# Decode attention with a gated MLP: which queue starts w1, x, b1 and b2, and when wq is issued

## The chip, the cores and the metric

The kernel runs on one core of a Trainium2 chip. The metric is the device time of one execution in microseconds (us). Data comes from HBM through 16 DMA engines that are shared by all queues of the core; SyncE (SP in the profile) and ScalarE (ACT) each issue transfers onto a queue of their own, `q1` and `q10` in the profile's numbering. That `q10` is ScalarE's can be seen from its contents: in the whole execution it holds 8 packets, which are the four rows of x, b1 and b2 and their four completions.

## What is computed

```python
x = A_x                                   # (2, 1, 512)
xn = layernorm(x)
q = xn @ wq                               # 32 heads of 128
p = softmax(q . k_cache / sqrt(128))      # k_cache, v_cache: (2, 32, 8192, 128) f32
s = (p . v_cache) @ wo
g = silu(gelu(layernorm(xn) @ w1 + b1) @ w2 + b2)   # w1: (512, 1376), w2: (1376, 512)
out = x + s * g
```

All is float32. The two caches are 512 MiB together, wq and wo 8 MiB each, w1 and w2 2.75 MB each.

## The kernel before

The caches are walked in 32 tiles of two heads: a K tile and a V tile are 128 partitions by 64 KB (8 MiB) each. VectorE multiplies a K tile with the broadcast query and reduces it (two passes), TensorE and ScalarE make the softmax, and TensorE multiplies the V tile. K has two buffers (`KBUF`, lines 107 to 109), V one (`VB`). `take("SP", "p_k")` and `take("SP", "p_free")` (lines 311 to 325) are SyncE's waits for a buffer to be free before it issues the next tile. Every operation is recorded by the helper `op` (lines 47 to 60), so the profile shows line 51 for nearly all of them; tiles tell them apart. The names `w1_sb`, `w2_sb`, `x_sb`, `xn`, `wo_sb` and others are views of the three large buffers `big`, and `wq_sb` is the second K buffer before it gets its first K tile, so their rows read `big<-in_B_w_dram`, `big<-in_A_x_dram` and so on.

Ahead of the loops stands a prologue, which the change touches. Lines 200 to 202: ScalarE issues x (two rows of 2 KB), b1 (one row of 5.5 KB) and b2 (one row of 2 KB). Lines 203 to 205: SyncE issues the last 96 lines of w2 (2 KB each), w1 (128 rows of 22,016 bytes, one for each partition) and wq (128 rows of 64 KB); line 212 the first K tile, line 213 the rest of w2. None of these waits for anything. VectorE clears PSUM banks and makes small masks out of an identity (lines 228 to 246), then runs `layernorm` (lines 251 to 260): statistics and their aggregation on VectorE, a square root on ScalarE, a reciprocal and the normalization on VectorE. Line 262 normalizes x, waiting for x's transfer; line 263 normalizes that once more for the MLP. TensorE transposes both, computes the hidden layer from w1, then q from wq (lines 435 to 441, event `pq`), spreads q over the partitions, and computes the gate from w2.

SyncE's later transfers hang on this: the second K tile (line 302) waits for `pq` and for wq's transfer, since it overwrites wq; the first V tile (lines 308 and 309) waits for the gate, since it overwrites w1, w2 and the rest of the third buffer. An engine's instructions run in their order, so a waiting SyncE issues nothing that is written behind the wait.

At the end come wo in eight transfers (lines 326 to 329), the last products, and the output's transfer.

Of the kernel before, what the change touches and what calls it, by code (L numbers as in the profile page):

```python
# [13 lines left out]
class Program:  # L14
# [32 lines left out]
    def op(self, eng, method, *args, waits=(), sig=None, by=1, quiet=False, **kwargs):  # L47
        need = self.need(eng, waits)
        for name, v in need[:-1]:
            self.engines[eng].wait_ge(self.sem(name), v)  # L50
        ins = getattr(self.engines[eng], method)(*args, **kwargs)  # L51
        for name, v in need[-1:]:
            ins._wait_ge(self.sem(name), v)
        if quiet:
            return None
        name = sig or "own_" + eng
        by = 16 if method == "dma_start" else by
        ins.then_inc(self.sem(name), by)
        self.counts[name] += by
        return name, self.counts[name]  # L60


def decode_kernel(nc, x, kc, vc, wq, wo, w1, b1, w2, b2, out):
    P = 128
# [18 lines left out]
    NF = F // P  # L83
# [12 lines left out]
    op, wait, take = pr.op, pr.wait, pr.take  # L96

    def sb(shape, name):
        return nc.alloc_sbuf_tensor(name, list(shape), F32).ap()
# [12 lines left out]
    def boot(p, n):  # L112
        a = used[0]
        used[0] += n
        assert used[0] <= KP * DH
        return big[2][:p, a:a + n]

    w1_sb = boot(P, ND * F).rearrange("p (c f) -> p c f", f=F)
    QN = big[2][:BH, 2 * 512:2 * 512 + N * DH].rearrange("h (n d) -> h n d", d=DH)
    w2_sb = boot(P, (NF + 1) * D).rearrange("p (c n) -> p c n", n=D)  # L120
    x_sb = boot(B, D)
    xn = boot(B, D)
    y = boot(B, D)
    b2_sb = boot(1, D)
    b1_sb = boot(1, F)
# [5 lines left out]
    wq_sb = big[1].rearrange("p (c n) -> p c n", n=H * DH)  # L131
# [59 lines left out]
    def pe(name):  # L191
        return "pe_setup", PE_EVENTS.index(name) + 1

    def pe_n(name, n):
        return name, n + 1

    t = {}


    t["x"] = op("ACT", "dma_start", x_sb, x.rearrange("b s d -> (b s) d"), sig="d_x")  # L200
    t["b1"] = op("ACT", "dma_start", b1_sb, b1[None, :], sig="d_b1")
    t["b2"] = op("ACT", "dma_start", b2_sb, b2[None, :], sig="d_b2")
    op("SP", "dma_start", w2_sb[:FT, NF, :], w2[NF * P:, :], sig="d_w2")
    op("SP", "dma_start", w1_sb, w1.rearrange("(p c) f -> p c f", p=P), sig="d_w1")
    op("SP", "dma_start", wq_sb, wq.rearrange("(p c) n -> p c n", p=P), sig="d_wq")

    def load_k(n, *waits):
        sems, cuts = ([f"d_k{n % U}", "d_kl"], HALVES) if n == N - 1 else ([f"d_k{n % U}"], (0, KP))
        for name, (c0, c1) in zip(sems, zip(cuts, cuts[1:])):
            op("SP", "dma_start", KBUF[n % U][:, c0:c1], kf[n][:, c0:c1], sig=name, waits=waits)  # L210

    load_k(0)
    t["w2"] = op("SP", "dma_start", w2_sb[:, :NF, :], w2[:NF * P, :].rearrange("(p c) n -> p c n", p=P), sig="d_w2")


    op("POOL", "memset", ones, 1.0)
# [12 lines left out]
    for k in (7, 6, 1, 2, 4, 0):  # L229
# [13 lines left out]
                  op=ALU.add)  # L243
    t["sel"] = op("DVE", "tensor_copy",
                  sel[:, HP:].rearrange("p (b j r) -> p b j r", b=B, r=HG)[:, :, :QT, 0], by_row[:, :B, :],
                  waits=[t["sel0"]])
# [4 lines left out]
    def layernorm(dst, src, name, after):  # L251
        st = sb([B, nc.vector.BN_STATS_DIM], f"st_{name}")
        mv = sb([B, nc.vector.BN_AGGR_DIM], f"mv_{name}")
        sd = sb([B, 2], f"sd_{name}")
        a = op("DVE", "bn_stats", st, src, waits=[after])
        a = op("DVE", "bn_aggr", mv, st, waits=[a])
        c = op("ACT", "activation", sd[:, 0:1], mv[:, 1:2], AF.Sqrt, bias=eps_t, scale=1.0, waits=[a])
        c = op("DVE", "reciprocal", sd[:, 1:2], sd[:, 0:1], waits=[c])
        return op("DVE", "tensor_scalar", dst, src, mv[:, 0:1], sd[:, 1:2], op0=ALU.subtract, op1=ALU.mult,
                  waits=[a, c])  # L260

    t["xn"] = layernorm(xn, x_sb, "xn", t["x"])
    t["y"] = layernorm(y, xn, "y", t["xn"])
    t["xnT"] = op("DVE", "tensor_copy", xnT, pxn.rearrange("p (c b) -> p c b", b=B), waits=[pe("xnT")])
    t["yT"] = op("DVE", "tensor_copy", yT, py.rearrange("p (c b) -> p c b", b=B), waits=[pe("yT")])
# [4 lines left out]
    c = op("DVE", "tensor_mul", gu, gh, gh, waits=[a])  # L270
    c = op("DVE", "tensor_scalar", gu, gu, GELU_A, 1.0, op0=ALU.mult, op1=ALU.add, waits=[c])
    c = op("DVE", "tensor_mul", gu, gu, gh, waits=[c])
    c = op("ACT", "activation", gu, gu, AF.Tanh, scale=GELU_C, waits=[c])
    c = op("DVE", "scalar_tensor_tensor", gu, gu, 1.0, gh, op0=ALU.add, op1=ALU.mult, waits=[c])
# [8 lines left out]
    for part, n0, n1 in (("first", 0, NPB), ("rest", NPB, N)):  # L283
# [3 lines left out]
                           waits=[t["qall"], t["mine"]])  # L287
# [15 lines left out]
    for b in range(B):  # L303
        t["x4"] = op("SP", "dma_start", x4[HB * b::R, :], x[b, 0].rearrange("(j n) -> j n", n=P), sig="d_x4",
                     waits=[t["x4m"]])
# [49 lines left out]
    with nc.scalar.Fori(0, N // U) as i:  # L355
        for u in range(U):
# [4 lines left out]
            for s in range(U):  # L361
# [11 lines left out]
                   waits=[t["th"], t["pool"]])  # L373
# [8 lines left out]
                 op=ALU.mult, waits=[t["rl"], t["on0"], pe_n("p_oa", 0)])  # L382
    t["wide"] = op("ACT", "copy", o4, pw, waits=[pe_n("p_w", 0)])
    a = op("DVE", "scalar_tensor_tensor", res, acc, 0.5, gate, op0=ALU.mult, op1=ALU.mult,
           waits=[pe_n("p_acc", 0), t["gate"]])
    t["res"] = op("DVE", "tensor_add", res, res, x4, waits=[a, t["x4"]])
    t["out"] = op("SP", "dma_start", out.rearrange("b s (j n) -> j (b s) n", n=P), res[::HB, :], sig="d_out",
                  waits=[t["res"]])
# [42 lines left out]
    for k in range(NH):  # L431
        n = min(QT, NF + 1 - k * QT)
# [9 lines left out]
    for n in range(NG // QT):  # L442
        for hh in range(HG):
# [3 lines left out]
               waits=[t["sel"], t["qnat"]], sig="pqa" if last else None)  # L447

    for g in range(N // NPB):
        mm(PB[g % len(PB)], sides, QN[:, g * NPB:(g + 1) * NPB, :].rearrange("h n d -> h (n d)"),  # L450
           waits=[t["side"], t["QN rest" if g else "QN first"]] + ([t[f"Q{QH}"]] if g >= len(PB) else []),
           sig=f"pb{g}")
    for f in range(NF + 1):
# [3 lines left out]
           waits=[t["hT"], t["w2"], t["mem6"]])  # L457
    mm(pg[R * (QT - 1):R * (QT - 1) + B, :], ones[:1, :B], b2_sb, start=False, stop=True, waits=[t["b2"]], sig="pg")
    for j in range(QT):
        mm(pgate[R * j:R * j + MB, :], mod_b[:, :MB], g_nat[:, j * P:(j + 1) * P], waits=[t["g"], t["mod_b"]],  # L460
           sig="pgate" if j == QT - 1 else None)
# [64 lines left out]
    for b in range(B):  # L526
        h = slice(b * H, (b + 1) * H)
        mm(OA[:, b, :OC], Z[:, h].rearrange("p h r -> p (h r)"), mod, waits=[t["Z"]],
           sig="p_oa" if b == B - 1 else None)
    unread(1)  # L530
    for i, (c0, c1) in enumerate(zip(WO_CUTS, WO_CUTS[1:])):
        for c in range(c0, c1):
            after = [t["on"], t["mem"], (f"d_wo{i}", 16)]
            if c < WIDE:
                j = c % QT
                mm(pw[R * j:R * j + MB, :], on[:, :, c], wo_sb[:, c, :], start=c < QT, stop=c + QT >= WIDE,
                   waits=after, sig="p_w" if c == WIDE - 1 else None)
# [7 lines left out]
        if c1 == OC - 2:  # L545
            for j in range(QT):
                mm(acc[R * j:R * j + MB, :], mod[:, :MB], o4[:, j * P:(j + 1) * P], start=False, stop=False,
                   waits=[t["wide"]])
# [26 lines left out]
```

## Time and profile before

| | us |
|---|---|
| median of 3 runs (1299.70 to 1301.15) | 1300.71 |
| time of the profiled execution | 1299.53 |
| its span | 1298.2 |

1.3 us of the profiled execution lie around its span. Over the span the 16 DMA engines moved 559.30 MB at 431 GB/s, VectorE was busy for 87% and TensorE for 36%. In the rows, "SPq" and "ACTq" are the issuing side of SyncE and ScalarE, `<-` behind a time names what ended an engine's idle time, and a DMA share of 1.00 is all 16 engines busy. The share of a very short window can pass 1, since a packet is counted where it begins.

### The profile page before, as it was taken

What the parts mean: (1) busy time and instruction counts of PE and PEld (TensorE: products, weight loads), DVE (VectorE), ACT (ScalarE), POOL (GpSimd) and SP (SyncE); (2) the same over time, 40 slices, a digit from 0 to 9 for tenths busy, and PEclk for the clock granted to TensorE, in tenths of its full rate; (3) what the DMA queues carried; (4) which work ended last, traced back from release to release, by engine and by line L of the source; (5) the groups of instructions that cost most, each with busy time, mean ns of one, the idle gap of its engine ahead of it and who ended that gap; (6) DMA issues with size and microseconds to landing.
All of it is one profiled execution on the core that took longest, in us unless ns stands there. A gap on an engine that the chain in (4) does not pass through costs nothing. (4 is left out here: it accounts for less than half of the span.)

```text
span 1298.2 us, 7420 instructions
## 1 busy us (share of the span) xinstructions
PE 465.6 (36%) x2958; PEld 150.8 (12%) x2958; DVE 1135.7 (87%) x171; ACT 81.1 (6%) x279; POOL 2.3 (0%) x15
## 2 busy tenths in 40 slices
PE   3813343323334322433322343322334321333338
PEld 1201111001111000111100111100111100111103
DVE  2599999988889988889988888988888988888991
ACT  1200000000000000000000000000000000000000
POOL 0000000000000000000000000000000000000000
PEclk8757766666776566677656767656776666677659
DMA  9999999999999999999999999999999999999998
GB/s 412 436 426 442 430 430 436 426 446 426 438 430 424 446 426 442 430 430 436 426 446 426 438 430 424 446 426 444 428 432 434 426 446 426 438 430 424 432 436 360
DMA packets 11241, 559.37 MB, mean 431 GB/s; under 512 B 1264, under 2 KB 1536, under 8 KB 1892
## 3 DMA queue, kind: packets, MB, share of 16 engines
q1 hardware_dynamic: 11228, 559.30, 99.7%
q8 instruction: 3, 0.05, 0.0%
q14 instruction: 2, 0.02, 0.0%
q10 hardware_dynamic: 8, 0.01, 0.0%
HBM read 559.30 MB, written 0.00 MB: 431 GB/s over the span
## 5 line engine op out<-in xcount | busy, mean ns | idle before, releaser
L51 DVE TENSOR_TENSOR big<-big,bank 128x16384 f32<-128x16384 f32 (+1 forms) x33 | 551.2, 16704 | 73.2 <-DVEq L45 73.2
L51 DVE TENSOR_REDUCE sc<-big 128x128 f32<-128x16384 f32 (+1 forms) x33 | 551.2, 16703 | 4.8
L51 PE MATMUL bank<-big,PZ 128*8 128x512 f32 x2048 | 293.0, 736 | 632.1 <-PEq L45 632.1
L51 PEld LDWEIGHTS bank<-big,PZ 128*8 128x8 f32 x2048 | 60.5, 103 | 837.3 <-issue 837.3
L51 PE MATMUL bank<-Q,ident 128*128 128x512 f32 (+2 forms) x198 | 79.8, 514 | 0.3 <-issue 0.3
L51 ACT COPY o<-bank 128x512 f32<-128x512 f32 x33 | 19.3, 586 | 887.3 <-ACTq L45 875.9
L51 PE MATMUL bank<-ident,MX 128*1 128x128 f32 x32 | 9.8, 308 | 132.8 <-PEq L45 132.8
L51 PE MATMUL bank<-mod,o 128*128 128x2 f32 x256 | 32.8, 250 | 27.4 <-PEq L45 27.4
L51 PEld LDWEIGHTS bank<-mod,o 128*128 128x128 f32 x256 | 31.0, 191 | 55.4 <-issue 55.4
L51 PEld LDWEIGHTS bank<-Q,ident 128*128 128x128 f32 x198 | 34.8, 205 | 16.5 <-issue 16.5
L51 ACT ACTIVATE PZ<-sc,bias 64x128 f32<-64x128 f32 x64 | 25.5, 399 | 6.6 <-ACTq L45 6.2
L51 DVE TENSOR_REDUCE nm<-bank 1x2 f32<-1x128 f32 x32 | 8.9, 279 | 19.4 <-DVEq L45 19.4
L51 DVE TENSOR_TENSOR big<-big,mine 64x512 f32<-64x512 f32 (+1 forms) x2 | 4.5, 2278 | 21.2 <-ACT big L51 21.2
L51 PEld LDWEIGHTS bank<-ident,MX 128*1 128x1 f32 x32 | 2.5, 79 | 157.8 <-issue 157.8
L51 ACT COPY bias<-bank 128x1 f32<-128x1 f32 x32 | 5.1, 159 | 220.2 <-ACTq L45 220.2
L51 PE MATMUL bank<-big,sides 64*128 64x512 f32 x16 | 12.8, 972 | 3.7 <-DVE big L51 3.7
L51 PE MATMUL bank<-nm,srow 1*64 1x1 f32 x128 | 10.4, 218 | 8.9 <-PEq L45 7.1
L51 DVE TENSOR_REDUCE MX<-sc 128x1 f32<-128x128 f32 x32 | 9.2, 286 | 4.7
L51 PE MATMUL bank<-big,xnT 128*2 128x512 f32 x64 | 9.0, 727 | 10.3 <-DMA big<-in_A_wq_dram 10.3
L51 ACT ACTIVATION_READ_ACCUMULATOR PZ<-sc,bias x64 | 11.8, 185 | 0.0
L51 PE MATMUL bank<-big,on 128*17 128x512 f32 (+1 forms) x88 | 10.8, 569 | 0.9 <-DMA big<-in_A_wo_dram 0.8
L51 DVE SCALAR_TENSOR_TENSOR res<-bank,gate 128x128 f32<-128x128 f32 x1 | 0.3, 291 | 11.9 <-PE bank L51 11.9
(80 smaller groups left out, 83.8 us busy)
## 6 DMA issues: line engine op xcount, KB each, us to landing
big<-in_A_k_cache_dram SPq DMA_DIRECT2D x2, 4096.0 KB, 35.9
big<-in_A_v_cache_dram SPq DMA_DIRECT2D x2, 4096.0 KB, 35.8
big<-in_B_w_dram SPq DMA_DIRECT2D x1, 2752.0 KB, 10.2
big<-in_B_w_dram SPq DMA_DIRECT2D x1, 2560.0 KB, 52.1
big<-in_A_wo_dram SPq DMA_DIRECT2D x1, 2560.0 KB, 15.0
big<-in_A_wo_dram SPq DMA_DIRECT2D x1, 2048.0 KB, 19.5
big<-in_A_wo_dram SPq DMA_DIRECT2D x1, 1536.0 KB, 22.7
big<-in_A_wo_dram SPq DMA_DIRECT2D x1, 1024.0 KB, 24.8
```

The costliest lines, as they stand in the source:

```text
L51: ins = getattr(self.engines[eng], method)(*args, **kwargs)
```

## The change

ScalarE issues one transfer only, w1, as its first instruction. SyncE issues w2's last lines as before, and behind them x, b1 and b2 on the same queue. wq, the first K tile and the rest of w2 move behind the first normalization in the program, still on SyncE's queue and in their old order, and wq gets a wait for that normalization's result `xn`. What is computed stays the same.

```diff
@@ -197,20 +197,17 @@
-    t["x"] = op("ACT", "dma_start", x_sb, x.rearrange("b s d -> (b s) d"), sig="d_x")
-    t["b1"] = op("ACT", "dma_start", b1_sb, b1[None, :], sig="d_b1")
-    t["b2"] = op("ACT", "dma_start", b2_sb, b2[None, :], sig="d_b2")
+    op("ACT", "dma_start", w1_sb, w1.rearrange("(p c) f -> p c f", p=P), sig="d_w1")
     op("SP", "dma_start", w2_sb[:FT, NF, :], w2[NF * P:, :], sig="d_w2")
-    op("SP", "dma_start", w1_sb, w1.rearrange("(p c) f -> p c f", p=P), sig="d_w1")
-    op("SP", "dma_start", wq_sb, wq.rearrange("(p c) n -> p c n", p=P), sig="d_wq")
+    t["x"] = op("SP", "dma_start", x_sb, x.rearrange("b s d -> (b s) d"), sig="d_x")
+    t["b1"] = op("SP", "dma_start", b1_sb, b1[None, :], sig="d_b1")
+    t["b2"] = op("SP", "dma_start", b2_sb, b2[None, :], sig="d_b2")
 
     def load_k(n, *waits):
...
-    load_k(0)
-    t["w2"] = op("SP", "dma_start", w2_sb[:, :NF, :], w2[:NF * P, :].rearrange("(p c) n -> p c n", p=P), sig="d_w2")
...
@@ -260,6 +257,9 @@
     t["xn"] = layernorm(xn, x_sb, "xn", t["x"])
+    op("SP", "dma_start", wq_sb, wq.rearrange("(p c) n -> p c n", p=P), sig="d_wq", waits=[t["xn"]])
+    load_k(0)
+    t["w2"] = op("SP", "dma_start", w2_sb[:, :NF, :], w2[:NF * P, :].rearrange("(p c) n -> p c n", p=P), sig="d_w2")
     t["y"] = layernorm(y, xn, "y", t["xn"])
```

## Rows read from the trace of the kernel before

**Rows 1.** The page: engines, DMA share in 40 slices, ScalarE's queue, w1's landing.
```profile
PE 465.6 (36%) x2958; PEld 150.8 (12%) x2958; DVE 1135.7 (87%) x171; ACT 81.1 (6%) x279; POOL 2.3 (0%) x15
DMA  9999999999999999999999999999999999999998
q10 hardware_dynamic: 8, 0.01, 0.0%
...
big<-in_B_w_dram SPq DMA_DIRECT2D x1, 2752.0 KB, 10.2
```

**Rows 2.** Windows by stage: window, length, engines' busy time, PEclk, DMA share, GB/s.
```profile
2.00:12.00 10.00, 1.09 (x8) 1.03 (x8) 6.73 (x23) 1.75 (x3) 0.91 (x5) 1.00 1.04 419
12.00:50.00 38.00, 22.09 (x141) 7.68 (x142) 5.57 (x8) 4.75 (x9) 0.00 (x0) 0.80 1.00 431
...
600.00:1230.00 630.00, 216.13 (x1399) 68.95 (x1392) 570.86 (x65) 35.23 (x130) 0.00 (x0) 0.67 1.00 433
```

**Rows 3.** Windows of the last transfers, columns as in Rows 2.
```profile
1293.00:1293.25 0.25, 0.25 (x8) 0.00 (x0) 0.00 (x0) 0.00 (x0) 0.00 (x0) 1.00 1.09 397
...
1293.75:1294.00 0.25, 0.06 (x5) 0.01 (x1) 0.00 (x0) 0.13 (x1) 0.00 (x0) 1.00 0.52 180
...
1294.50:1294.90 0.40, 0.40 (x24) 0.37 (x16) 0.00 (x0) 0.00 (x0) 0.00 (x0) 1.00 0.14 49
```

**Rows 4.** Timeline, K and V transfers: start, length, engine, line, what, idle before.
```profile
30.84 9.04 PE L51 MATMUL bank<-big,xnT 128*2 128x512 f32 x64 [10.26 <-DMA big<-in_A_wq_dram]
40.02 0.33 SPq L51 DMA_DIRECT2D big<-in_A_k_cache_dram  x1
65.76 0.34 SPq L51 DMA_DIRECT2D big<-in_A_v_cache_dram  x1
87.00 0.35 SPq L51 DMA_DIRECT2D big<-in_A_k_cache_dram  x1
95.09 9.35 PE L51 MATMUL bank<-big,PZ 128*8 128x512 f32 x64 [8.32 <-PEq L45]
```

**Rows 5.** Timeline of the prologue: the issues, and the first normalization.
```profile
0.74 0.55 ACTq L51 DMA_DIRECT2D big<-in_A_x_dram  x1
0.74 0.88 SPq L51 DMA_DIRECT2D big<-in_B_w_dram  x2
1.32 0.53 ACTq L51 DMA_DIRECT2D big<-in_B_b_dram  x2
1.66 1.94 SPq L51 DMA_DIRECT2D big<-in_A_wq_dram  x1
3.65 0.43 SPq L51 DMA_DIRECT2D big<-in_A_k_cache_dram  x1
5.72 0.68 DVE L51 BATCH_NORM_STATS2 st_xn<-big 2x6 f32<-2x512 f32 x1
7.15 0.53 DVE L51 TENSOR_SCALAR big<-big,mv_xn,sd_xn 2x512 f32<-2x512 f32 x1
12.08 5.59 PE L51 MATMUL bank<-big,yT 128*2 128x384 f32 x40 [0.35 <-DVE yT L51]
21.96 0.18 DVE L51 TENSOR_SCALAR hT<-gu 128x22 f32<-128x22 f32 x1
```

**Rows 6.** Queues (packets, MB, share) in 1.6 to 1.9, 4.9 to 5.1, 5.8 to 5.9.
```profile
q1 hardware_dynamic: 8, 0.02, 32.9%
q8 instruction: 1, 0.02, 30.2%
q10 hardware_dynamic: 4, 0.00, 5.1%
...
q1 hardware_dynamic: 6, 0.13, 154.3%
q10 hardware_dynamic: 1, 0.00, 2.6%
...
q1 hardware_dynamic: 1, 0.02, 51.1%
q10 hardware_dynamic: 1, 0.00, 0.6%
```

## What the change was predicted to do

> **What bounds the kernel now.** I read the page first: VectorE is busy for 87% of the span, but the 16 DMA engines stand at 9 in 39 of 40 slices, and in the last at 8 [rows 1]. The windows by stage say it more sharply: from the prologue to the end of the loops the DMA share is 1.00 or a little more, at 419, 431 and 433 GB/s [rows 2]. So nothing that an engine computes sets the time; the DMA engines do, from their first byte to the last of wo. The timeline shows why they never run dry in the loops. The second K tile is issued at 40.02 and the first V tile at 65.76; the next K tile goes onto the queue at 87.00, while the V tile before it is used only from 95.09 on [rows 4]. At 433 GB/s a tile of 8.39 MB takes 19.4 us, so each issue comes some 8 us before the engines would be idle. **Thus the rule for this change**: an instant in which a DMA engine idles ahead of wq is paid in full at the end, and one microsecond saved there is gained in full. Everything behind wq keeps its order: q's products start when wq has landed (30.84), the second K tile is issued behind them (40.02) [rows 4], and all of that moves with wq by the same amount, the queue being as full as before.
>
> **The DMA engines in the prologue before.** Issues start at 0.74 on both queues, x on ScalarE's and w2's last lines and w1 on SyncE's; wq is issued from 1.66 and the K tile from 3.65 [rows 5]. x is on the engines early: in 1.6 to 1.9 us ScalarE's queue has four of its eight packets, two rows and two completions [rows 6]. That is 0.86 to 1.16 us behind x's issue; I take 1.0 us from the start of an issue to its first packet. VectorE clears banks until 5.72 and then normalizes without any wait for x; the result is written at 7.15 + 0.53 = 7.68 [rows 5]. The chain from x to `xn` is 7.68 - 5.72 = 1.96 us. Ahead of wq lie w1 (2.82 MB), w2's last lines (0.20 MB) and some 0.03 MB of the rest: 3.05 MB, 7.3 us at 419 GB/s [rows 2]. From a first packet at about 1.7 this ends at 9.0 on average; w1's last row landed 10.2 us behind its issue at 0.74 to 1.18 [rows 1, 5], so the slowest engine ended at 10.9 to 11.4. For most engines I take **9.5**, an estimate nearer to the lower end, since few engines are late [rows 3]. wq's rows have long been queued by then, so no engine waits.
>
> **What the change costs, step by step.**
> (1) w1 on ScalarE's queue: one issue at 0.74 instead of three of 1.08 us together [rows 5]. w1's first rows come up to half a microsecond sooner, but w2's last lines now share the engines with them; the bytes ahead of wq are the same, so w1 is done at about 9.4, and this part is worth 0 to -0.3 us. The hidden layer begins at 12.08 behind the second normalization, not behind w1, so w1's landing isn't what it waits for [rows 5].
> (2) x behind w2's last lines. x's issue moves from 0.74 to 0.74 + 0.44 = 1.18, by half of the 0.88 us that the two issues took [rows 5]. That half microsecond is nothing by itself: x has until 5.72. What matters is how a DMA engine shares itself between w1's rows on one queue and the short rows on the other. Before, b2 stood in just that place: ScalarE's last issue ended at 1.32 + 0.53 = 1.85 [rows 5], and with the same 1.0 us (counted from the middle of that double issue, 1.59) its row would be due at about 2.6. Its row is in the window of 4.9 to 5.1, and its completion in the one of 5.8 to 5.9 [rows 6]. A row of w1 takes 22,016 bytes / (433 GB/s / 16) = 0.81 us on one engine; the completion thus came one w1 row behind the data that directly preceded it, and the data 2.4 us, or three such rows, late. I read this as one packet from each queue in turn. On the engines that carry x, SyncE's queue now holds six of w2's 96 lines (96 / 16), their completion, x's row and x's completion, that is nine packets, against eight rows of w1 (128 / 16) and a completion on ScalarE's. In turns, x's completion stands behind all eight rows of w1: about 1.7 + 1.2 (the first row, taken half as long again) + 7 x 0.81 + 8 x 0.08 = **9.2**. It can't be much later, since w1 is then done; it can be as early as 5.72 or sooner at no cost, if the short rows pass. I take 9.3.
> (3) The wait. `xn` is ready at 9.3 + 1.96 = 11.3; SyncE sees it some 0.1 later, issues wq, and the first packets follow 1.0 to 1.6 us behind (1.0 as above, and up to 0.6 more for the engine served last: in 1.6 to 1.9 only 8 packets of w2's lines had come to 16 engines [rows 6]). wq's rows so begin at 12.4 to 13.0 instead of about 9.5: **+2.9 to +3.5 us** for an engine that was early before. Queued behind the waiting wq on SyncE are the first K tile and the rest of w2; neither can fill the gap. b1 and b2 are ahead of it and are only 7.5 KB.
> (4) The restart. The engines stop and start again; how slow first rows are no row shows by itself. I bound it by 0 and the 0.8 us of one whole w1 row, and take nearly the middle, **+0.35**.
> (5) What the stop gives back. The engines don't end together: their share is 1.09 in 1293.00 to 1293.25, 0.52 in 1293.75 to 1294.00 and 0.14 in 1294.50 to 1294.90 [rows 3], so the last two or three end over a microsecond behind the bulk. One source of such a lag is seen in the prologue: an instruction load on `q8` takes one engine's time at 1.6 to 1.9 [rows 6]. As the engines never wait afterwards, a lag from the prologue is kept to the end. A stop before wq lets the late ones catch up. Bounds are 0 and 1.2 us; I take **-0.8**.
> The sum is 2.9 to 3.5, so 3.1, then + 0.35 - 0.8 - 0.15 = **+2.5 us**. On the profiled execution (1299.53) that is 1302.0; the median of the runs is 1.18 us higher, and on it the sum gives **1303.2**, +0.19%. What hides the rest: the hidden layer, its activation (`hT` done at 21.96 [rows 5]) and the second normalization all come 3.6 us later, but q's products wait for wq until 30.84 [rows 4], 8.9 us behind `hT`, and wq moves too.
>
> On the turns a rule of the Trainium skill speaks otherwise. The row on b2 shows one w1 row between b2's data and its completion, which follow each other on the same queue [rows 6]. DMA: Bandwidth & Descriptors, section "Queues, rings and completion order", says that an engine drains a whole packet, typically 9 to 17 descriptors, of one queue before it switches. By that rule the nine short packets ahead of and with x would be one turn, and the sum would be rival 1's instead of +2.5 us; b2's completion speaks against it, as data and completion would not have been parted.
>
> **Rivals.**
> *1. x passes w1, and nothing changes.* If the short packets of SyncE's queue go in one turn, or w2's lines are through before w1's first rows come, x is there by 2.7 to 5.7. Then `xn` is ready at 7.68 as before, wq is issued at about 7.8 and its rows queue from 8.8 to 9.4, just before w1 ends at 9.4. Shift -0.5 to +0.6 us, **1300.7**. For it: x's two rows are ready to go by 2.2 and need only 0.08 us each. Against it: b2 [rows 6].
> *2. Clearly slower: wq's issue itself is long.* The only issue of wq in the trace took 1.94 us, while K tiles with rows of the same size took 0.33 to 0.43 [rows 4, 5]. Before, that was hidden behind w1's 7 us; now nothing stands behind it. If the rows reach the engines only as the issue goes on, the last engine starts 1.5 us later than in (3), and the kernel takes +4 us, **1304.7**. The same happens if x's engine is one delayed by an instruction load. It decides from an issue above 0.9 us on. Against it: the length coincides with the instruction load that starts before 1.9, which the new order has long behind it when wq is issued.
> *3. Faster.* w1's earlier first rows (-0.3) and the engines' catching up (-0.8 at most), with x early enough that no gap arises: -0.6 to -1.1, **1299.8**. The catching up needs a stop, though, so both together are unlikely.
>
> **How the numbers follow.** About 0.2% of this kernel, 2.6 us, is what a measurement can tell from no change. My forecast has 0.60, with a range of its own from +1.6 to +3.3 us (1302.3 to 1304.0) from the bounds in (2) to (5); of it 0.26 lies above 2.6 us. Rival 1 has 0.20, rival 2 0.16, rival 3 0.04, of which 0.02 faster than 0.2% is already generous. Slower: 0.26 + 0.16 = 0.42; faster 0.02; same 0.56. The range goes from rival 1's lower part, 1300.2, to the middle of rival 2, 1304.8; outside are about 0.08 above and 0.07 below.
>
> **What would show it.** x's completion at 8.4 to 9.4 (statistics start right behind it) supports (2); statistics at 5.72 as before mean rival 1. SyncE's wq row at about 11.4 with a length near 0.4 supports (3), one near 1.9 rival 2. The DMA share between about 9.5 and 12.5 should fall near zero; wq's products should start at 33.0 to 33.8 instead of 30.84, and every later issue, the last of wo included, should be late by 2 to 3 us. If the gap is there and the end doesn't move, the rule of the first part is wrong. If the statistics start late and the DMA share stays at 1, I have mistaken what is queued ahead of wq.

## The result and the profile after

The changed kernel takes 1303.35 us (median of 10 runs, 1303.00 to 1304.24) against 1300.25 us (10 runs) of the kernel before: a ratio of 1.0025, 95% interval 1.0016 to 1.0033, that is +3.1 us. Forecast were +2.5 us and 1303.2. The profiled execution took 1304.09 us, one of the three longest of the ten; a second profile of the same code, taken with the experiments below, took 1303.51.

What the change did is read from the prologue. The timeline of the changed kernel (start, length, engine, line, what; in brackets the idle time before and what ended it) answers to [rows 4, 5]:

```profile
0.74 0.41 ACTq L51 DMA_DIRECT2D big<-in_B_w_dram  x1
0.74 0.41 SPq L51 DMA_DIRECT2D big<-in_B_w_dram  x1
1.22 0.31 SPq L51 DMA_DIRECT2D big<-in_A_x_dram  x1
...
9.53 0.68 DVE L51 BATCH_NORM_STATS2 st_xn<-big 2x6 f32<-2x512 f32 x1 [3.71 <-DMA big<-in_A_x_dram]
...
10.97 0.53 DVE L51 TENSOR_SCALAR big<-big,mv_xn,sd_xn 2x512 f32<-2x512 f32 x1
11.53 0.36 SPq L51 DMA_DIRECT2D big<-in_A_wq_dram  x1
11.93 0.43 SPq L51 DMA_DIRECT2D big<-in_A_k_cache_dram  x1
...
35.39 9.58 PE L51 MATMUL bank<-big,xnT 128*2 128x512 f32 x64 [12.32 <-DMA big<-in_A_wq_dram]
45.10 0.33 SPq L51 DMA_DIRECT2D big<-in_A_k_cache_dram  x1
```

x is issued at 1.22 and VectorE stands for 3.71 us until it lands at 9.53, where it never waited before. `xn` is there at 11.50, and SyncE, whose next instruction waits for it, issues wq at 11.53 instead of 1.66. Everything behind wq is later too.

The DMA share over the same stretch (windows: window, length, busy time of PE, PEld, DVE, ACT and POOL, PEclk, DMA share, GB/s), and below it three long windows that answer to [rows 2]:

```profile
9.50:10.00 0.50, 0.00 (x0) 0.00 (x0) 0.47 (x1) 0.00 (x0) 0.00 (x0) 1.00 0.31 103
10.00:11.00 1.00, 0.00 (x0) 0.00 (x0) 0.57 (x4) 0.29 (x1) 0.00 (x0) 1.00 0.16 66
11.00:12.50 1.50, 0.61 (x4) 0.55 (x4) 1.35 (x3) 0.04 (x1) 0.00 (x0) 1.00 0.04 11
12.50:13.00 0.50, 0.00 (x0) 0.00 (x0) 0.18 (x2) 0.25 (x1) 0.00 (x0) 1.00 5.46 1835
...
2.00:16.00 14.00, 2.70 (x23) 1.92 (x26) 6.74 (x23) 1.05 (x3) 0.92 (x5) 1.00 0.92 348
16.00:46.00 30.00, 16.02 (x112) 3.99 (x102) 1.09 (x6) 2.94 (x5) 0.00 (x0) 0.72 0.99 426
46.00:1290.00 1244.00, 438.26 (x2750) 141.90 (x2752) 1126.29 (x137) 75.70 (x271) 0.00 (x0) 0.67 1.00 433
```

The same three long windows of the kernel before:

```profile
2.00:16.00 14.00, 5.00 (x42) 2.88 (x45) 6.73 (x23) 1.75 (x3) 0.91 (x5) 1.00 1.07 441
16.00:46.00 30.00, 16.09 (x109) 4.99 (x102) 3.70 (x8) 4.01 (x8) 0.00 (x0) 0.77 0.99 430
46.00:1290.00 1244.00, 439.57 (x2752) 141.22 (x2752) 1123.64 (x136) 74.61 (x268) 0.00 (x0) 0.67 1.00 433
```

The engines stand nearly still from 10 to 12.5 us. Then fourteen rows of wq begin in one half microsecond (1835 GB/s x 0.5 us / 64 KB). Up to 46 us the changed kernel is behind by (93 GB/s x 14 us + 4 GB/s x 30 us) / 433 GB/s = 3.3 us of transfer; from there to 1290 us both run at 433 GB/s. The loss happens once, in the prologue, and up to 1290 us these windows show nothing that adds to it or takes from it. A window counts a packet where it begins, so such a sum is good to about half a microsecond.

### The profile page after: what moved, and what is told of

Its sections match the earlier page's. It is cut to its first block, busy times and chain, and to the rows that moved or that the text cites. A ratio compares the mean times of both kernels' runs of the same rounds, so it can differ in the third digit from the quotient of the medians.

```text
span 1302.8 us, 7420 instructions
## 1 busy us (share of the span) xinstructions
PE 464.8 (36%) x2958; PEld 150.1 (12%) x2958; DVE 1135.7 (87%) x171; ACT 81.1 (6%) x279; POOL 2.3 (0%) x15
## 5 line engine op out<-in xcount | busy, mean ns | idle before, releaser
L51 PEld LDWEIGHTS bank<-nm,srow 1*64 1x64 f32 x128 | 8.6, 164 | 15.6 <-issue 15.6
## 6 DMA issues: line engine op xcount, KB each, us to landing
big<-in_B_w_dram ACTq DMA_DIRECT2D x1, 2752.0 KB, 11.4
```

## Experiments

The theory: on each DMA engine w1's rows and SyncE's short rows take turns, packet by packet; so x comes late, so `xn` does, so wq does, and the time in which the DMA engines idle is paid in full at the end. Its rivals are that the wait, or w1's new queue, costs by itself; that x waits for the whole of w1 whatever stands in front of it; and that a gap is partly made up for later.

**The wait taken away.** wq is issued as soon as SyncE comes to it; all else as in the changed kernel.

```diff
-    op("SP", "dma_start", wq_sb, wq.rearrange("(p c) n -> p c n", p=P), sig="d_wq", waits=[t["xn"]])
+    op("SP", "dma_start", wq_sb, wq.rearrange("(p c) n -> p c n", p=P), sig="d_wq")
```

> The changed kernel with one thing undone: wq's transfer no longer waits for the first normalization (its place in the program and w1 on ScalarE's queue stay). Theory (the gap ahead of wq is what costs, nothing else): x is still late, statistics at 8.5 to 11 us, but the DMA engines never idle and the time goes back to the kernel before, 1300.3 +- 0.7 us. Rival (w1 on ScalarE's queue, or the late normalization by itself, costs): stays at 1302.5 to 1303.5.

Measured: 1301.12 us (11 runs, 1300.36 to 1301.94), ratio to the kernel before 1.0007 (0.9998 to 1.0016). Its timeline:

```profile
2.13 0.36 SPq L51 DMA_DIRECT2D big<-in_A_wq_dram  x1
9.68 0.68 DVE L51 BATCH_NORM_STATS2 st_xn<-big 2x6 f32<-2x512 f32 x1 [3.87 <-DMA big<-in_A_x_dram]
31.83 9.09 PE L51 MATMUL bank<-big,xnT 128*2 128x512 f32 x64 [3.60 <-DMA big<-in_A_wq_dram]
```

x is as late as in the changed kernel (9.68), and it costs little: q's products start at 31.83. So neither the late normalization nor w1's queue is what costs the 3 us; wq's late issue is. The median lies 0.1 us above the range expected.

**x first.** x is issued ahead of w2's last lines; the wait stays.

```diff
-    op("SP", "dma_start", w2_sb[:FT, NF, :], w2[NF * P:, :], sig="d_w2")
     t["x"] = op("SP", "dma_start", x_sb, x.rearrange("b s d -> (b s) d"), sig="d_x")
+    op("SP", "dma_start", w2_sb[:FT, NF, :], w2[NF * P:, :], sig="d_w2")
```

> The changed kernel with x ahead of w2's last lines on SyncE's queue; the wait stays. Theory (turn about between the two queues holds x back, the wait turns that into a gap): x lands by 3 us, statistics at 5.72, wq issued at 7.8, its first rows at 8.8 to 9.4 and so before w1 is done: 1300.3 us, from 1299.7 to 1301.0. Rival (the wait costs in any case, as a restart of the queue): 1302 to 1303.

Measured: 1301.09 us (11 runs, 1300.17 to 1302.23), ratio 1.0007 (0.9998 to 1.0016). The timeline:

```profile
5.72 0.67 DVE L51 BATCH_NORM_STATS2 st_xn<-big 2x6 f32<-2x512 f32 x1
7.71 0.36 SPq L51 DMA_DIRECT2D big<-in_A_wq_dram  x1
8.11 1.10 SPq L51 DMA_DIRECT2D big<-in_A_k_cache_dram  x1
```

Exchanging two lines gives back 2.3 of the 3.1 us. The wait alone, with x early, ends at 7.71 as worked out before. The median lies 0.1 us above the range expected.

**Turns, or whole queues: two tests.** In the first, w1 is loaded in two transfers of half a row each (11,008 bytes), in the same order:

```diff
-    op("ACT", "dma_start", w1_sb, w1.rearrange("(p c) f -> p c f", p=P), sig="d_w1")
+    for c in range(0, ND, 2):
+        op("ACT", "dma_start", w1_sb[:, c:c + 2], w1.rearrange("(p c) f -> p c f", p=P)[:, c:c + 2], sig="d_w1")
...
-               start=c == 0, stop=False, waits=[t["yT"], t["mem7"], ("d_w1", 16)])
+               start=c == 0, stop=False, waits=[t["yT"], t["mem7"], ("d_w1", 32)])
```

The last two lines make the hidden layer wait for both transfers.

> The changed kernel with w1 issued in two transfers of half the columns chunks each, so that a row on the DMA queue has 11,008 bytes instead of 22,016; the order and the wait stay. Theory (one packet from each queue in turn, whatever its size): x stands behind as many rows, each half as long; 7 or 8 rows of 0.41 instead of 0.82 us, so x lands at about 5.5 to 6.5, statistics at 5.7 to 6.5, and the time is 1300.0 to 1301.2. Rival (a queue is drained whole before the other, or the share goes by bytes): x lands at 8.9 to 9.5 as in the changed kernel and the time stays at 1303.0 to 1303.7.

In the second, w1 stays as it is and x stands between two halves of w2's last lines:

```diff
-    op("SP", "dma_start", w2_sb[:FT, NF, :], w2[NF * P:, :], sig="d_w2")
+    op("SP", "dma_start", w2_sb[:FT // 2, NF, :], w2[NF * P:NF * P + FT // 2, :], sig="d_w2")
     t["x"] = op("SP", "dma_start", x_sb, x.rearrange("b s d -> (b s) d"), sig="d_x")
+    op("SP", "dma_start", w2_sb[FT // 2:FT, NF, :], w2[NF * P + FT // 2:, :], sig="d_w2")
```

> The changed kernel with x between two halves of w2's last lines: 48 lines (three rows on each engine) before x, 48 behind it. Theory (one packet from each queue in turn): three of w2's rows fewer ahead of x mean three of w1's rows fewer as well, 3 x 0.9 us = 2.7 us: statistics at 6.6 to 7.1 instead of 9.5, wq issued at 8.6 to 9.1, time 1300.7 to 1301.4. Rival (x waits until w1 is through, however many packets are ahead of it): statistics at 9.2 or later, 1303.0 or more.

The statistics' row of the kernel with w1's rows halved:

```profile
6.88 0.68 DVE L51 BATCH_NORM_STATS2 st_xn<-big 2x6 f32<-2x512 f32 x1 [1.07 <-DMA big<-in_A_x_dram]
```

and of the kernel with half of w2's lines ahead of x:

```profile
6.76 0.68 DVE L51 BATCH_NORM_STATS2 st_xn<-big 2x6 f32<-2x512 f32 x1 [0.94 <-DMA big<-in_A_x_dram]
```

The times are 1301.03 us (11 runs; 1.0006, 0.9997 to 1.0015) and 1301.11 us (11 runs; 1.0007, 0.9998 to 1.0016). x comes 2.65 us sooner when w1's rows are half as long, and 2.77 us sooner when three rows fewer of w2 stand in front of it on each engine, against the 9.53 of the changed kernel. The second lies inside what was expected (6.6 to 7.1), the first 0.4 us above its range. The number of packets ahead of x, times the length of a packet on the other queue, sets when x lands. Had x waited for w1 as a whole, it would have come at 9 us in both. If a turn were one whole transfer, x would follow w1's first half in the first test, which fits 6.88; the second test, where w1 is a single transfer, speaks against that. In the changed kernel the turns can be counted too. From 3 to 7 us as many rows of w1 begin on ScalarE's queue as packets on SyncE's (queue: packets, MB, share):

```profile
q10 hardware_dynamic: 64, 1.41, 89.2%
q1 hardware_dynamic: 63, 0.13, 9.2%
```

**The wait doubled.** wq, the first K tile and the rest of w2 stand behind the second normalization, and wq waits for its result.

```diff
     t["xn"] = layernorm(xn, x_sb, "xn", t["x"])
-    op("SP", "dma_start", wq_sb, wq.rearrange("(p c) n -> p c n", p=P), sig="d_wq", waits=[t["xn"]])
+    t["y"] = layernorm(y, xn, "y", t["xn"])
+    op("SP", "dma_start", wq_sb, wq.rearrange("(p c) n -> p c n", p=P), sig="d_wq", waits=[t["y"]])
     load_k(0)
...
-    t["y"] = layernorm(y, xn, "y", t["xn"])
```

> The changed kernel with the wait doubled: wq, the first K tile and the rest of w2 stand behind the second normalization, and wq waits for y, which is 2.0 us later than xn in the trace. Theory (each microsecond that the DMA engines idle ahead of wq is paid in full at the end): +2.0 us over the changed kernel, 1305.1 to 1305.6. Rival (part of a gap is made up for later, by buffers that are free early or engines that catch up): 1303.4 to 1304.6.

Measured: 1305.48 us (5 runs, 1305.14 to 1305.67), ratio 1.0039 (1.0025 to 1.0053). The timeline:

```profile
10.06 0.68 DVE L51 BATCH_NORM_STATS2 st_xn<-big 2x6 f32<-2x512 f32 x1 [4.25 <-DMA big<-in_A_x_dram]
14.05 0.36 SPq L51 DMA_DIRECT2D big<-in_A_wq_dram  x1
```

Two windows of it, columns as above (share and GB/s last):

```profile
13.00:15.00 2.00, 0.64 (x4) 0.55 (x4) 0.92 (x4) 0.27 (x1) 0.00 (x0) 1.00 0.00 0
15.00:15.50 0.50, 0.43 (x4) 0.14 (x8) 0.00 (x0) 0.00 (x0) 0.00 (x0) 1.00 6.39 2097
```

wq's issue moved from 11.53 to 14.05 in the traces, 2.5 us, of which 2.0 are the second normalization and 0.5 that x came later in this execution. The distance to the kernel before grew from 3.1 and 3.3 us (the two comparisons of the changed kernel) to 5.4, by 2.1 to 2.3 us. Within a few tenths, a microsecond of gap is a microsecond at the end; the rival's 1303.4 to 1304.6 us, with part of the gap made up for, was not met.

**The parts alone.** First the wait in the kernel before, with x, b1 and b2 left on ScalarE's queue and w1 on SyncE's:

```diff
-    op("SP", "dma_start", wq_sb, wq.rearrange("(p c) n -> p c n", p=P), sig="d_wq")
...
-    load_k(0)
-    t["w2"] = op("SP", "dma_start", w2_sb[:, :NF, :], w2[:NF * P, :].rearrange("(p c) n -> p c n", p=P), sig="d_w2")
...
     t["xn"] = layernorm(xn, x_sb, "xn", t["x"])
+    op("SP", "dma_start", wq_sb, wq.rearrange("(p c) n -> p c n", p=P), sig="d_wq", waits=[t["xn"]])
+    load_k(0)
+    t["w2"] = op("SP", "dma_start", w2_sb[:, :NF, :], w2[:NF * P, :].rearrange("(p c) n -> p c n", p=P), sig="d_w2")
```

> The kernel before with one part of the change alone: wq, the first K tile and the rest of w2 move behind the first normalization, and wq waits for xn; x, b1 and b2 stay on ScalarE's queue, w1 on SyncE's. The two earlier kernels without a gap ahead of wq (wait removed; x first) still stood some 0.9 us above the kernel before. Theory A (that rest comes from w1 and SyncE's rows sharing the engines from two queues): x is early, wq is issued at 7.8 and queues behind w1 on the same queue, so 1300.1 +- 0.3 us. Theory B (the rest comes from the wait, wq's rows coming late): 1300.8 to 1301.3.

Then the queues alone: the changed kernel with x first and without the wait.

> The other parts alone: w1 is ScalarE's first load, x, w2's last lines, b1 and b2 are on SyncE's queue with x first, and nothing waits for xn. Theory A (two queues sharing the engines cost some 0.9 us): 1300.8 to 1301.3 us. Theory B (the wait costs that): 1300.1 +- 0.3; if w1's earlier first rows are worth what was estimated, 1299.8.

Measured: 1301.07 us (11 runs, 1299.95 to 1301.73; 1.0005, 0.9996 to 1.0014) for the wait, 1300.97 us (11 runs, 1300.01 to 1302.08; 1.0005, 0.9996 to 1.0014) for the queues. The test was to say which of the two carries a rest of 0.9 us, and it does not: both stand 0.7 to 0.8 us above the kernel before, each within its interval of no difference. The wait ends as worked out, in time for w1's end:

```profile
7.71 0.33 SPq L51 DMA_DIRECT2D big<-in_A_wq_dram  x1
8.09 1.28 SPq L51 DMA_DIRECT2D big<-in_A_k_cache_dram  x1
31.77 8.92 PE L51 MATMUL bank<-big,xnT 128*2 128x512 f32 x64 [11.07 <-DMA big<-in_A_wq_dram]
```

**Is the rest an offset of the comparison?** The kernel before was timed against itself in the place of the others.

> The kernel before, timed against itself in the place where the others were timed. Five kernels that leave no long gap ahead of wq stood 0.7 to 1.0 us above the kernel before, with intervals that include no difference; their traces account for 0.2 to 1.0 us each. If this offset belongs to the comparison, it is 0.5 us or more here too; if it belongs to the kernels, 0.0 +- 0.3 us.

Measured: 1299.97 against 1299.99 us, ratio 1.0001 (0.9992 to 1.0010). There is no offset. Six kernels without a long gap ahead of wq (wait taken away, x first, halved rows, halved lines, wait alone, queues alone) have medians of 1300.97 to 1301.12 us, 0.7 to 1.1 us above the kernel before in their comparisons, so a loss of that size is likely, though each interval alone includes none. What it consists of was not settled; one part of it shows in the first rows of wq (step (4) below).

**w2's last lines out of the way.** In the kernel with x first, they were put behind the first K tile, so that w1 has the engines nearly to itself:

```diff
-    op("SP", "dma_start", w2_sb[:FT, NF, :], w2[NF * P:, :], sig="d_w2")
...
     load_k(0)
+    op("SP", "dma_start", w2_sb[:FT, NF, :], w2[NF * P:, :], sig="d_w2")
```

> The changed kernel with x first and w2's last 96 lines behind the first K tile, so that w1 has the engines nearly to itself until wq; the wait stays. If the short rows of w2 between w1's rows are what costs 0.9 us in the kernel with x first: 1300.1 +- 0.4 us. If the change from one queue to the other (wq's first rows beside w1's last ones) costs it: 1300.8 to 1301.3.

Measured: 1302.33 us (11 runs, 1301.65 to 1303.91), ratio 1.0017 (1.0007 to 1.0026). Neither expectation was met: it is slower by 1.2 us than with the lines beside w1. The windows show a second place of loss. This kernel, 49 to 53 us:

```profile
49.00:53.00 4.00, 3.29 (x4) 1.50 (x5) 0.97 (x2) 0.58 (x1) 0.00 (x0) 0.50 0.94 303
```

The same window in the kernel before:

```profile
49.00:53.00 4.00, 4.00 (x6) 1.65 (x5) 2.72 (x1) 1.33 (x3) 0.00 (x0) 0.50 1.01 435
```

Here the 2 KB rows come behind the 64 KB rows of K and ahead of the 20 KB rows of w2's rest. The engines are busy (0.94) and move 303 GB/s, where a share of 0.94 at the steady 433 GB/s is worth 407: 104 x 4 / 433 = 1.0 us lost, for a transfer whose bytes are worth 0.45 us. The two stretches don't hold the same rows, so this price is approximate; but the share beside the rate says that the engines were occupied, not idle. In the prologue these rows are cheaper: beside w1 (1301.09 us, x first), or in front of it (the kernel before).

**The changed kernel once more.**

> The changed kernel once more, on the chip of these experiments: 1303.3 +- 0.5 us. In its profile one DMA engine got its first wq row 1.2 us behind all others, beside an instruction load; if that is chance, a second profile shows the last engine closer to the rest, and a time near 1303.1 rather than 1304.1.

Measured: 1303.51 us (9 runs, 1302.97 to 1304.49), ratio 1.0024 (1.0014 to 1.0034); this profile's own execution took 1303.51. Its rows:

```profile
11.76 0.36 SPq L51 DMA_DIRECT2D big<-in_A_wq_dram  x1
33.62 9.27 PE L51 MATMUL bank<-big,xnT 128*2 128x512 f32 x64 [10.34 <-DMA big<-in_A_wq_dram]
```

wq was issued 0.23 us later than in the first profile and yet had landed 1.77 us sooner. The queue of instruction loads shows what differed. In the first profile, 12.0 to 12.5 us, right ahead of wq's first rows:

```profile
q8 instruction: 1, 0.02, 10.9%
```

In the second, the same load began in 10.5 to 11.0, within the gap:

```profile
q8 instruction: 1, 0.02, 14.5%
q10 hardware_dynamic: 3, 0.02, 10.4%
```

Two profiles make it plausible that an instruction load that meets wq's start costs one engine about a microsecond, and that the longest runs (1304.0 and more) are of this kind. It is not shown; no run varied that load alone.

## Why the prediction was right, and where a step failed

**What bounds the kernel: right.** The gap lies in the first 13 us, the rate behind it is unchanged, and doubling the wait moved the end by about as much as the second normalization lasts (2.1 to 2.3 us against 2.0).

**x behind w2's lines, step (2): right, in mechanism and size.** Predicted were 9.2 to 9.3 by turns, and 8.4 to 9.4 as the sign of it; the statistics began a little later, at 9.53 and 9.76 in two profiles of the changed kernel. The one row of b2 on which it rested [rows 6] carried it. The two tests with half the row length and half of w2's lines moved x by 2.65 and 2.77 us, and the rows that begin on the two queues are equal in number (64 and 63). The Trainium skill's rule (DMA: Bandwidth & Descriptors, section "Queues, rings and completion order") is that a whole packet of one queue, typically 9 to 17 descriptors, is drained before the engine turns to another queue. With w1 as one transfer of eight rows on each engine, that would have had x pass with w2's lines, or wait for all of w1; x's landing at 6.76 us fits neither, nor do the equal numbers, and the measurement decides here.

**The wait, step (3): right.** wq's issue came at 11.53 (about 11.4 was worked out) and its rows began from 12.5 on (12.4 to 13.0). wq's products began at 33.62 in the second profile (33.0 to 33.8), and at 35.39 in the first, where one engine's row of wq came late. Rival 2, the long issue, fell: it took 0.36 us. Rival 1 is what the kernel with x first does, nearly: 1301.09 against 1300.7 worked out.

**Step (1): no gain was seen.** I credited 0 to -0.3 us for w1's earlier start. The queues alone (1300.97) gave no gain, and a loss if anything; the interval (0.9996 to 1.0014) is too wide to rule out 0.3 us.

**The restart, step (4): too small.** Fourteen rows of wq beginning in 12.5 to 13.0 carry 5.46 x 0.5 us x 16 engines = 43.7 us of packet time, 3.1 us each; the sixteen of the kernel with the wait doubled took 6.39 x 0.5 us = 3.2 us each. At the steady rate a 64 KB row takes 65,536 / (433 GB/s / 16) = 2.42 us. The first rows thus cost 0.7 us more, where I took 0.35; the bounds held (0 to 0.8). That the pause is the reason is not shown. The kernel with w1's rows halved has none (w1's rows alone make a share of 0.99 in 9.0 to 9.5 us), and yet the first five rows of wq, in 9.5 to 10.0, took 1.951 x 0.5 us x 16 / 5 = 3.1 us each:

```profile
q1 hardware_dynamic: 5, 0.33, 195.1%
```

**What the stop gives back, step (5): failed.** I took -0.8 us, because the engines end apart from each other [rows 3] and I ascribed that to lags from the prologue that a stop would wipe out. The tail of the second profile of the changed kernel says otherwise:

```profile
1297.00:1297.50 0.50, 0.50 (x8) 0.00 (x0) 0.00 (x0) 0.00 (x0) 0.00 (x0) 1.00 0.99 334
1297.50:1298.00 0.50, 0.29 (x4) 0.00 (x0) 0.00 (x0) 0.14 (x1) 0.00 (x0) 1.00 0.33 107
1298.00:1298.50 0.50, 0.50 (x17) 0.41 (x17) 0.00 (x0) 0.45 (x1) 0.00 (x0) 1.00 0.07 25
1298.50:1299.00 0.50, 0.50 (x26) 0.41 (x20) 0.00 (x0) 0.00 (x0) 0.00 (x0) 1.00 0.04 12
```

The share falls from 0.99 to 0.04 within 1.5 us, as it fell from 1.09 to 0.14 before. The ends are as far apart as they were, so nothing was given back there. The first half of the argument held, though: the stop did draw the engines together. In the loops each engine begins a 64 KB row every 2.42 us, and how far apart the sixteen begin shows the lags. In the kernel before, thirteen begin in 1104.05 to 1104.75 us and three in 1104.75 to 1105.65:

```profile
q1 hardware_dynamic: 13, 0.85, 281.0%
...
q1 hardware_dynamic: 3, 0.20, 50.5%
```

In the second profile of the changed kernel all sixteen begin in 1108.00 to 1108.70. Near the end of the loops it is fifteen in 1255.65 to 1256.35, and one in 1256.35 to 1257.25:

```profile
q1 hardware_dynamic: 16, 1.05, 346.0%
...
q1 hardware_dynamic: 15, 0.98, 324.4%
...
q1 hardware_dynamic: 1, 0.07, 16.8%
```

So one engine fell behind again after the lags of the prologue were gone. Between the two stretches lies one instruction load, on the queue `q14`, in 1222.0 to 1222.5:

```profile
q14 instruction: 1, 0.01, 4.2%
```

It may be what set that engine back; no run varied it. What failed is that the engines, once together, would stay so to the end.

With 0 for step (5) and 0.7 for step (4) the sum would have been 3.1 + 0.7 - 0.15 = 3.65 us; measured were 3.1 in the first comparison and 3.3 in the second (1303.51 against 1300.23). The forecast of +2.5 thus owes its closeness in part to luck: two of its small terms were taken too favourably by 1.15 us together, and the rest of the sum was 0.35 to 0.55 us too high. Of that, about 0.2 us is the gap itself, which is wider for engines that were early than for the late ones, and 3.1 was counted from an early one. By the bytes in half-microsecond windows, eleven, three and two of wq's first rows begin in those from 9.5 to 11.0 us in the kernel before; in the changed kernel fourteen, one and one begin in those at 12.5, 13.0 and 14.0. Put at the middle of their windows, that is 9.97 and 12.88 us on the mean, 2.9 us apart. What the remaining 0.15 to 0.35 us are was not settled.

The chances leaned the wrong way by a little: "within 0.2%" was given 0.56 and "slower" 0.42, and the ratio of 1.0025 lies just on the slower side.

## What to carry to other kernels

In a kernel that moves data without a pause, a wait on the issuing engine costs little as long as queued bytes outlast it (0.7 to 1.1 us here, in no run clear of no difference), and about its full length from there on. So the transfer that such a wait hangs on goes first on its queue. A small transfer behind n short packets, with long rows on another queue, landed about n long rows later here (n up to eight), however few bytes stood in front of it.

## What the runs showed that was not expected

- After a pause the first 64 KB rows took 3.1 us each, against 2.42 at the steady rate, when 14 of them began within half a microsecond; in the kernel with w1's rows halved the first five took as long without a pause.
- 96 rows of 2 KB between rows of 64 and of 20 KB cost about 1 us with the engines at a share of 0.94; their bytes are worth 0.45 us.
- A stop in the prologue drew the sixteen engines together for more than a thousand microseconds; one of them was behind again at the end, and no gain was seen.
- The length of an issue depends on where it stands: wq's took 1.94 us right behind w1's on SyncE's queue [rows 5] and 0.36 us after the wait, while the first K tile's took 0.43 and, in the kernel with x first, 1.10.
